# Two more output buffers taken from the first expert's token tile, and a flag word loaded without its bounds check

## The chip, the cores and the metric

The kernel runs on one core of a Trainium2 chip. A core has five engines that work side by side, each with its own queue of instructions: TensorE (PE, matrix products), VectorE (DVE), ScalarE (ACT), GpSimd (POOL) and SyncE (SP, which issues most of the DMAs). They wait for one another by semaphores. The metric is the device time of one execution in microseconds (us), lower is better.

## The reference

Attention, then a mixture of experts. The attention (4 batches, 8 heads, 768 positions, 64 dimensions) is masked: a query sees the keys that fall to the same of 16 centroids. Its output, 3072 tokens of 512 numbers, goes through a two-level router that sends each token to one of 16 experts with one gate per token; the expert is a two-layer net:

```python
for g in range(G):                    # 4 groups of 4 experts
    ...
    for e in range(Eg):
        mask_e = e_idx == e
        h = np.maximum(xg[mask_e] @ w1[g, e], 0.0)   # 512 -> 1024
        ye = h @ w2[g, e]                            # 1024 -> 512
        combined = g_w[mask_g][mask_e] * e_w[mask_e]
        out[tok_idx] = combined[:, None] * ye
```

## The kernel before

Attention takes the first 405 us; the experts, which overlap its end, take the rest. Each expert's tokens are gathered from DRAM by index, multiplied, and scattered to their rows of the output by index.

**The experts.** One expert, chosen early ("the first expert"), is computed in a part A with 256 tokens (line 1183) as soon as most of attention is done; its last tokens follow in a part B of at most 104 rows. The function `bridge` runs part A's second layer beside part B's first. The other 15 experts are sorted by their number of tokens, and `ranks` runs them as ranks 0 to 14, the fullest first (288 tokens for rank 0, then 272, 256, 240, 232, ...). In each round the first layer (`up`, matmuls of line 1064 into `psh`) of rank k is interleaved with the second layer (`down`, lines 1098 or 1122 into `psy`) of rank k-1.

Numbers are split into a high and a low 16-bit half, so that three 16-bit products stand for one of higher precision. Hence the names: `hh` and `hl` are the two halves of the hidden values, written from `psh` by ACT (line 1069) and then by DVE (line 1070); `wh..` and `wl..` are the two halves of a weight matrix, made of a loaded 512 KB chunk `st` by ACT (line 833) or POOL (line 835) and then by DVE (line 836). SP loads the chunks (line 826); some are loaded straight into weight buffers that are not yet in use.

**Outputs.** The function `emit` (line 1160) finishes one tile of up to 128 tokens: ACT scales PSUM by the gate into a buffer `y` of 128 x 512 in fp32 (line 1163), and POOL issues an indirect DMA that scatters its rows to the output (line 1164). `y` has three buffers, used in turn; a write to one waits until the DMA that read it three tiles earlier has landed. There are 35 such tiles: two for part A, one for part B, three each for ranks 0 and 1 (the third one of 32 and of 16 rows), and two for every other rank. Ranks in the `down` form of line 1098 keep their results (`owed`) until `settle`, in the round after, turns them through the `psm` tiles of line 1150 and emits them one behind the other; rank 2, with two tiles, has the form of line 1122 and emits each tile when its sum is finished.

**Order.** From the second half of `bridge` to the last rank the order on PE, ACT and DVE is that of the program text (`manual_schedule`); an instruction that waits holds everything behind it on its engine. POOL and SP are placed by a planner. `widen` (line 1160's change asks for it) is false in the bridge and in the first round and true from round 1 on, which is where rank 0's tiles are emitted; `again` is true only in a path for tokens left over, which this data does not enter.

**The first expert's tokens.** `fetch` (lines 905 to 944) puts part A's 256 tokens, transposed, into the tile `xTA`: 128 partitions with 4 x 2 x 256 fp16 numbers, that is 4096 bytes each. Part A's first layer reads it; its last matmul of that kind starts at 403.5 us.

**The word of flags.** For most ranks the program holds two versions of each group of matmuls, a wide and a narrow one, and PE branches between them (line 1304) by a bit of a register `word`. At step 5 of the bridge's second loop (line 1457) `values_load` loads this register on PE from SBUF. With it come instructions that test the value against its declared bounds.

Of the kernel before, what the change touches and what calls it, by code (L numbers as in the profile page):

```python
# [14 lines left out]
F32 = mybir.dt.float32  # L15
# [4 lines left out]
ET = mybir.EngineType  # L20
# [4 lines left out]
P = 128  # L25
# [720 lines left out]
class Experts:  # L746
# [155 lines left out]
    def fetch(self):  # L902

        nc, R, CA, KD = self.nc, self.R, self.CA, self.R.KD
        nt = -(-CA // P)
        sz = [min(P, CA - t * P) for t in range(nt)]
        tab = self.small("tabA", [P, nt, 2])
        tv = R.table.rearrange("(e s) w -> e s w", s=R.BS)[bass.ds(self.f0, 1)].rearrange("e s w -> (e s) w")
        self.nt = -(-max(self.caps) // P)
        self.tb = self.small("tb", [R.E, self.nt * P, 2])  # L910
        while R.done < R.B - 2:
            yield
        for _ in range(READ + 2):
            yield
        with self.after(), self.tc.issue_after(self.cfg["mr"].ins) if "mr" in self.cfg else ExitStack():
            for t, n in enumerate(sz):
                R.reads(nc.sync.dma_start(out=tab[0:n, t], in_=tv[t * P:t * P + n]))
            R.reads(nc.sync.dma_start(out=self.tb, in_=R.table.rearrange("(e s) w -> e s w", s=R.BS)[0:R.E, 0:self.nt * P]))
        for _ in range(READ):
            yield  # L920
        ids = self.small("idA", [P, nt], I32)
        g = self.small("gA", [P, nt])
        with self.after():
            for t, n in enumerate(sz):
                nc.vector.tensor_copy(out=ids[0:n, t:t + 1], in_=tab[0:n, t, 0:1])
                nc.vector.tensor_scalar(out=g[0:n, t:t + 1], in0=tab[0:n, t, 1:2], scalar1=1.0 / (XS * WS * WS), scalar2=None, op0=ALU.mult)
        self.colsA = [g[0:n, t:t + 1] for t, n in enumerate(sz)], [ids[0:n, t:t + 1] for t, n in enumerate(sz)]

        rows = R.N - R.N // R.B
        xgs = []  # L930
        for t, n in enumerate(sz):
            xf = self.cfg["ld"].tile([P, KD * P * 3 // 2], F32, name=("qx", "kx", "vx")[t])[:, 0:self.D]
            nc.vector.memset(xf, 0.0)
            xgs.append(xf.bitcast(F16).rearrange("p (k a x) -> p k a x", a=2, x=P))
            if rows:
                with self.tc.issue_after(self.cfg["los"][0].ins) if "los" in self.cfg else ExitStack():
                    self.gather(ids[0:n, t:t + 1], n, xgs[t], rows)
            for _ in range(2):
                yield
        xTA = self.wa.tile([P, KD, 2, CA], F16, name="xTA")  # L940
        self.xTA = xTA.rearrange("p k a m -> p a k m")
        for t, n in enumerate(sz):
            nc.sync.dma_start_transpose(out=xTA.rearrange("p k a m -> p (k a) m")[:, :, t * P:t * P + n], in_=xgs[t][0:n].rearrange("p k a x -> p (k a x)"))
            yield

    def open(self, ctx):
        tc = self.tc
        late = ctx.enter_context(tc.tile_pool(name="econst2", bufs=1))
        self.small = lambda name, shape, dt=F32: late.tile(shape, dt, name=name)
        self.stage2 = ctx.enter_context(tc.tile_pool(name="stage2", bufs=2))  # L950
        wp = ctx.enter_context(tc.tile_pool(name="wp", bufs=1))
        self.W = [[self.wtiles(wp, 0, n) for n in "ab"], [self.WA[2:4], self.wtiles(wp, 1, "b")]]
        self.xp = ctx.enter_context(tc.tile_pool(name="mxp", bufs=2))
        self.pinned, self.left, self.widen = False, None, False
        self.owed, self.wrote, self.again = [], [], False
        self.back = late.tile([P, P], F16, name="back")
        self.nc.vector.tensor_scalar(out=self.back, in0=self.cfg["ident"], scalar1=YS, scalar2=None, op0=ALU.mult)
        self.ps_y = ctx.enter_context(tc.tile_pool(name="ps_y", bufs=2, space=PSUM))
# [200 lines left out]

    def emit(self, py, n, g, idc):  # L1160
        nc = self.nc
        y = self.xp.tile([P, self.D], F32, name="y", bufs=3)
        nc.scalar.activation(out=y[0:n], in_=py[0:n, 0:self.D], func=AF.Copy, scale=g)  # L1163
        d = self.put = nc.gpsimd.indirect_dma_start(  # L1164
            out=self.out, out_offset=bass.IndirectOffsetOnAxis(ap=idc, axis=0),
            in_=y[0:n], in_offset=None, bounds_check=self.R.N - 1, oob_is_err=False)
        if self.again:
            self.R.behind(d, self.wrote)
        else:

            self.R.alone(d, "wrote", self.wrote)
# [263 lines left out]
    def bridge(self, ga, new):  # L1435

        for i in range(8):
            next(ga)
            with self.tc.issue_after(self.mm.ins):
                if i >= self.ADD:  # L1440
                    next(new, None)
        self.pinned = True
        with self.tc.manual_schedule(engines=PINNED):
            h = []
            up = None
            for i in range(8):
                next(ga)
                if self.left:
                    self.left()
                    self.left = None  # L1450
                for _ in range((2, 1, 0, 1)[i] if i < 4 else 0):
                    next(new, None)
                if i == 0:
                    self.xTB = self.tokens_b()
                    up = self.up(self.xTB, self.CB, self.WA[0:2], h)
                if i == 5:
                    self.word = self.nc.values_load(self.wi[0:1, 0:1], engines=[ET.PE], min_val=0, max_val=2 ** self.R.E - 1)
                for _ in range(self.BESIDE[i]):
                    next(up)
                if i == self.SLOTS:  # L1460
                    self.slots()
                if i >= self.SLOTS:
                    next(self.fill)
            for _ in ga:
                pass
            xT = self.tokens(self.xg0, self.caps[0])
            for _ in up:
                next(self.fill)
            self.settle()
        return xT, self.xg0, None, self.down(h, self.CB, self.WA[2:4], [self.gB], [self.idB])  # L1470
# [238 lines left out]
```

## Time and profile before

| | |
|---|---|
| time, 3 runs | median 713.98 us (713.72 to 715.66) |
| profiled execution | 716.25 us, of which its span (first to last instruction) 714.4 us |
| busy share of the span | PE 96%, DVE 81%, ACT 70%, POOL 64% |
| mean granted TensorE clock | 0.992 |
| chain that ended last | PE 64%, DVE 14%, ACT 9%, DMA 6%, issue 5% |
| DMA | 136.74 MB, mean 191 GB/s |

All times of the rows below are microseconds from the start of the span. A duration in a row is that of the group of like instructions that the row stands for, and "x12" is their number. "Idle before" is how long the engine had nothing to do before that instruction, and the name behind the arrow is what ended this idle time. "issue" is idle time in which the engine waited for nothing that the profile shows. A row of a stretch holds, after its length, the busy time of PE, PEld (PE's weight loads), DVE, ACT and POOL with their numbers of instructions, then the granted clock as a share of 2.4 GHz, the busy share of the 16 DMA engines, and GB/s. A queue name with a q (SPq, PEldq) stands for instructions that the engine's sequencer carries out itself.

### The profile page before, as it was taken

How to read it: one execution, taken by the hardware profiler on the slowest of the kernel's cores; microseconds unless marked ns; L12 is line 12 of the kernel's file. 1: busy time of each engine (PE TensorE's matmuls, PEld its weight loads, DVE VectorE, ACT ScalarE, POOL GpSimd, SP SyncE). 2: the span in 40 equal slices, each digit the busy share in tenths (PEclk: the TensorE clock that was granted, in tenths of full speed). 3: DMA queues.
4: the chain of work that ended last, by engine and by line, in shares of the span. 5: the costliest groups of instructions: out<-in, count | busy, mean ns of one | idle time of the engine just before them, and what ended most of it. 6: DMA issues, size and time to landing. Idle time of an engine off the chain costs nothing.

```text
span 714.4 us, 25953 instructions
## 1 busy us (share of the span) xinstructions
PE 683.5 (96%) x10528; PEld 585.7 (82%) x10528; DVE 581.4 (81%) x1226; ACT 500.5 (70%) x948; POOL 459.4 (64%) x522
## 2 busy tenths in 40 slices
PE   5989999999999999999999989999899999999996
PEld 3667887887788887887778857898599999999995
DVE  5998989899798998989887836768488788888961
ACT  5558898897888978977996336665446666667642
POOL 9768888899988999989985032324524254453442
PEclk9999999999999999999999999999999999999998
DMA  8765737557486474552755179899789899888721
GB/s 254 201 176 158 201 89 189 136 125 196 96 167 157 110 203 100 116 120 52 167 119 106 61 265 313 283 353 226 279 257 293 272 289 302 300 286 294 217 78 48
DMA packets 89528, 136.74 MB, mean 191 GB/s; under 512 B 41508, under 2 KB 59428, under 8 KB 89385
## 3 DMA queue, kind: packets, MB, share of 16 engines
q1 hardware_dynamic: 83884, 121.32, 61.0%
q0 software_dynamic: 5344, 13.38, 5.6%
q8 instruction: 102, 1.67, 1.0%
q14 instruction: 42, 0.34, 0.2%
q10 hardware_dynamic: 156, 0.03, 0.0%
HBM read 93.17 MB, written 13.99 MB: 150 GB/s over the span
## 4 chain that ended last, share of the span: by engine, by line
PE 64%; DVE 14%; ACT 9%; DMA 6%; issue 5%; POOL 1%; SPq 1%; POOLq 0%; ACTq 0%; DVEq 0%
PE psh L1064 15%; PE psy L1098 14%; PE pso L395 10%; PE psc L320 6%; PE psf L362 5%; PE psf L363 5%; DVE mpart L323 5%; ACT p L367 3%; PE psy L1122 2%; PE psm L253 2%; DMA xT<-xg 1%; PE psm L1150 1%; PE psm L1032 1%; DMA vx<-vr 1%; DMA out_dram<-y,ri 1%
## 5 line engine op out<-in xcount | busy, mean ns | idle before, releaser
L374 POOL TENSOR_TENSOR pl<-p 128x512 f16<-128x512 f32 x193 | 198.8, 1055 | 20.3 <-ACT p L367 19.1
L323 DVE TENSOR_REDUCE mpart<-psc 128x1 f32<-128x512 f32 (+1 forms) x282 | 188.4, 681 | 17.8 <-PE psc L320 16.0
L367 ACT ACTIVATE p<-psf 128x512 f32<-128x512 f32 x288 | 171.8, 599 | 41.5 <-PE psf L363 33.6
L395 PE MATMUL pso<-V,pl 128*128 128x65 f16 (+1 forms) x1968 | 161.0, 193 | 0.0
L362 PE MATMUL psf<-A 82*128 82x384 f16 (+2 forms) x576 | 143.9, 274 | 2.3 <-ACT p L367 0.8
L363 PE MATMUL psf<-B 128*128 128x384 f16 (+2 forms) x576 | 143.7, 274 | 0.0
L395 PEld LDWEIGHTS <-pl 128*128 128x128 f16 x1968 | 130.9, 97 | 1.8 <-issue 0.4
L395 PEld LDWEIGHTS <-p 128*128 128x128 bf16 x1632 | 112.4, 98 | 20.3 <-issue 0.5
L395 PE MATMUL pso<-V,p 128*128 128x65 f16 x1632 | 120.8, 193 | 0.0
L374 POOL TENSOR_TENSOR pl<-p,ph 128x512 f16<-128x512 f32 x84 | 96.8, 1161 | 24.8 <-POOL pl L374 9.6
L320 PE MATMUL psc<-A 80*128 80x512 f16 (+1 forms) x376 | 107.6, 331 | 4.4 <-DVE mpart L323 3.0
L1069 ACT ACTIVATE hh<-psh 128x256 f16<-128x256 f32 (+14 forms) x136 | 46.1, 346 | 79.6 <-PE psh L1064 61.6
L1022 POOL DMA_INDIRECT xg<-xbuf,ri x32 | 35.1, 1098 | 84.2 <-PE psm L1032 38.4
L1070 DVE SCALAR_TENSOR_TENSOR hl<-psh,hh 128x256 f16<-128x256 f32 (+14 forms) x136 | 47.0, 365 | 36.3 <-ACT hh L1069 34.1
L1064 PE MATMUL psh<-xT,wh0a 128*128 128x272 f16 (+14 forms) x512 | 66.0, 246 | 3.2 <-DVE hl L1070 3.0
L363 PEld LDWEIGHTS <-B 128*128 128x128 f16 x576 | 56.8, 99 | 13.5 <-issue 4.1
L362 PEld LDWEIGHTS <-A 82*128 82x128 f16 x576 | 56.0, 98 | 10.3 <-issue 1.8
L1064 PE MATMUL psh<-xT,wl0a 128*128 128x272 f16 (+7 forms) x256 | 59.5, 245 | 0.0
L1064 PE MATMUL psh<-xT,wh0b 128*128 128x272 f16 (+6 forms) x448 | 57.2, 245 | 0.1
L1164 POOL DMA_INDIRECT out_dram<-y,ri x32 | 40.2, 1256 | 22.1 <-ACT y L1163 14.9
L371 ACT CAST ph<-p 128x512 f16<-128x512 f32 x84 | 51.9, 617 | 2.3
L1064 PE MATMUL psh<-xT,wl0b 128*128 128x240 f16 (+6 forms) x224 | 52.3, 244 | 0.0
(328 smaller groups left out, 1607.8 us busy)
## 6 DMA issues: line engine op xcount, KB each, us to landing
st<-w SPq DMA_DIRECT2D x88, 512.0 KB
B<-parts SPq DMA_DIRECT2D x64, 192.0 KB
wh<-w SPq DMA_DIRECT2D x21, 512.0 KB
wl<-w SPq DMA_DIRECT2D x19, 512.0 KB
kx<-kT SPq DMA_DIRECT2D x16, 384.0 KB
qx<-qT SPq DMA_DIRECT2D x16, 384.0 KB
vx<-vr SPq DMA_DIRECT2D x16, 384.0 KB
A<-parts SPq DMA_DIRECT2D x32, 192.0 KB
```

The costliest lines, as they stand in the source:

```text
L320: last["mm"] = nc.tensor.matmul(out=pc[:, off:off + k1 - k0], lhsT=QA[h % 8][0:80, c * P:(c + 1) * P], rhs=KA[h % 8][0:80, k0:k1], start=T ...
L323: nc.vector.tensor_reduce(out=(mp[:, 0, 0:1], mp[:, :, 1], mp[:, 1, 0:1])[i], in_=pc.rearrange("p (a x) -> p a x", a=n), axis=AX.X, op=ALU ...
L362: nc.tensor.matmul(out=o, lhsT=KA[h % 8][0:82, ks], rhs=QA[h % 8][0:82, q0:q1], start=True, stop=False)
L363: nc.tensor.matmul(out=o, lhsT=KBs[h][:, ks], rhs=QBs[h][:, q0:q1], start=False, stop=True)
L367: cfg["exp"] = nc.scalar.activation(out=p32, in_=pf, func=AF.Exp, scale=QK / (SQ * SQ))
L371: nc.scalar.copy(out=ph, in_=p32)
L374: lo = (nc.vector if u in (EARLY if h < 2 else DVE_LO[h % 8] if h < NH - 2 else DVE_END[h - NH]) else nc.gpsimd).tensor_tensor(out=pl, in0 ...
L395: nc.tensor.matmul(out=O[:, col:col + v.shape[-1]], lhsT=p[:, bs], rhs=v, start=c == 0 and q == 0 and i == 0, stop=c == NCH - 1 and i == l ...
L1064: self.mm = nc.tensor.matmul(out=ph[:, 0:n], lhsT=w[:, k, f * P:(f + 1) * P], rhs=xT[:, a, k, 0:n], start=i == 0, stop=i == 3 * KD - 1)
L1069: nc.scalar.activation(out=hh[:, f], in_=ph[:, 0:M], func=AF.Relu)
L1070: self.ev = nc.vector.scalar_tensor_tensor(out=hl[:, f], in0=ph[:, 0:M], scalar=0.0, in1=hh[:, f], op0=ALU.max, op1=ALU.subtract)
L1098: self.mm = nc.tensor.matmul(out=py[:, 0:n], lhsT=w[:, f, d * P:(d + 1) * P], rhs=a[:, f, 0:n], start=i == 0, stop=i == len(prods) - 1)
```

## The change

The first of four edits gives the bytes of `xTA` a second view, two buffers of 128 x 512 in fp32. The second adds a counter of emitted tiles. By the third, `emit` uses these two views for every tile whose number is 0 or 1 modulo 5, once `widen` is true, and the three old buffers for the others; a buffer then comes round after five tiles in place of three. No memory is added. By the fourth, the load of the word of flags is made without the check of its bounds.

```diff
--- before.py
+++ after.py
@@ -939,6 +939,7 @@
                 yield
         xTA = self.wa.tile([P, KD, 2, CA], F16, name="xTA")
         self.xTA = xTA.rearrange("p k a m -> p a k m")
+        self.yown = xTA.rearrange("p k a m -> p (k a m)").bitcast(F32)[:, 0:2 * self.D].rearrange("p (t d) -> p t d", d=self.D)
         for t, n in enumerate(sz):
             nc.sync.dma_start_transpose(out=xTA.rearrange("p k a m -> p (k a) m")[:, :, t * P:t * P + n], in_=xgs[t][0:n].rearrange("p k a x -> p (k a x)"))
             yield
@@ -951,7 +952,7 @@
         wp = ctx.enter_context(tc.tile_pool(name="wp", bufs=1))
         self.W = [[self.wtiles(wp, 0, n) for n in "ab"], [self.WA[2:4], self.wtiles(wp, 1, "b")]]
         self.xp = ctx.enter_context(tc.tile_pool(name="mxp", bufs=2))
-        self.pinned, self.left, self.widen = False, None, False
+        self.pinned, self.left, self.widen, self.ny = False, None, False, 0
         self.owed, self.wrote, self.again = [], [], False
         self.back = late.tile([P, P], F16, name="back")
         self.nc.vector.tensor_scalar(out=self.back, in0=self.cfg["ident"], scalar1=YS, scalar2=None, op0=ALU.mult)
@@ -1159,7 +1160,11 @@
 
     def emit(self, py, n, g, idc):
         nc = self.nc
-        y = self.xp.tile([P, self.D], F32, name="y", bufs=3)
+        self.ny += 1
+        if self.widen and not self.again and self.ny % 5 < 2:
+            y = self.yown[:, self.ny % 5]
+        else:
+            y = self.xp.tile([P, self.D], F32, name="y", bufs=3)
         nc.scalar.activation(out=y[0:n], in_=py[0:n, 0:self.D], func=AF.Copy, scale=g)
         d = self.put = nc.gpsimd.indirect_dma_start(
             out=self.out, out_offset=bass.IndirectOffsetOnAxis(ap=idc, axis=0),
@@ -1454,7 +1459,7 @@
                     self.xTB = self.tokens_b()
                     up = self.up(self.xTB, self.CB, self.WA[0:2], h)
                 if i == 5:
-                    self.word = self.nc.values_load(self.wi[0:1, 0:1], engines=[ET.PE], min_val=0, max_val=2 ** self.R.E - 1)
+                    self.word = self.nc.values_load(self.wi[0:1, 0:1], engines=[ET.PE], min_val=0, max_val=2 ** self.R.E - 1, skip_runtime_bounds_check_because="a sum of distinct powers of two below 2 ** E")
                 for _ in range(self.BESIDE[i]):
                     next(up)
                 if i == self.SLOTS:
```

## Rows read from the trace of the kernel before

**Rows 1.** Busy time in stretches (us, instructions), granted clock, DMA share

```profile
420.00:440.00 20.00, 16.78 (x152) 12.14 (x151) 12.24 (x20) 11.73 (x21) 8.72 (x8) 0.91 0.79 264
...
500.00:520.00 20.00, 16.99 (x140) 12.14 (x138) 10.55 (x14) 9.13 (x17) 10.76 (x11) 0.98 0.75 260
...
540.00:600.00 60.00, 59.94 (x753) 59.52 (x751) 49.49 (x77) 39.13 (x73) 24.63 (x28) 1.00 0.92 292
```

**Rows 2.** Waits of PE from 405 us on: us, times, longest

```profile
PE psh L1064 <- issue: 3.2, 6, 1.1
PE psh L1064 <- DVE hl L1070: 3.0, 1, 3.0
```

**Rows 3.** The chain of waits, 495 to 560 us: start, us, what

```profile
505.22 7.39 DMA out_dram<-y,ri
...
512.69 0.07 ACT y L1163
...
518.21 1.38 PE psh L1064 x12
519.59 3.76 PE psy L1098 x24
...
525.51 2.23 PE psy L1098 x24
```

**Rows 4.** ACT in order of time, 500 to 522 us: start, us, what

```profile
506.73 0.37 ACT L1069 ACTIVATE hh<-psh 128x240 f16<-128x240 f32 x1 [0.75 <-issue]
512.69 0.69 ACT L1163 ACTIVATE y<-psy,rg 128x512 f32<-128x512 f32 x1 [5.58 <-DMA out_dram<-y,ri]
...
515.17 0.62 ACT L1069 ACTIVATE hh<-psh 128x240 f16<-128x240 f32 x2
```

**Rows 5.** PE in order of time, around 504 us

```profile
504.08 0.38 PE L1122 MATMUL psy<-wh1b,hl 128*128 128x512 f16 x1
```

**Rows 6.** PE in order of time, around 515 us

```profile
511.27 0.26 PE L1064 MATMUL psh<-xT,wl0b 128*128 128x216 f16 x1
...
514.94 0.25 PE L1064 MATMUL psh<-xT,wl0a 128*128 128x208 f16 x1
```

**Rows 7.** Forms of line 836: duration in ns, least, median, most

```profile
L836 DVE SCALAR_TENSOR_TENSOR wl0b<-wl,wh0b x4: 1210/1216/3480, 514.4 to 629.0; 128x1024 f16<-128x1024 f32 x4
```

**Rows 8.** POOL in order of time, 508 to 520 us

```profile
514.66 2.10 POOL L835 TENSOR_SCALAR wh1b<-st 128x1024 f16<-128x1024 f32 x2
```

**Rows 9.** Busy time in the two stretches at half clock

```profile
427.03:430.45 3.42, 3.42 (x29) 2.83 (x28) 3.18 (x5) 2.77 (x6) 0.15 (x1) 0.50 0.70 196
...
519.19:522.60 3.41, 3.41 (x22) 2.88 (x20) 3.41 (x6) 2.25 (x3) 0.00 (x0) 0.50 0.85 260
```

**Rows 10.** Line 1457, what PE's sequencer did: duration in ns, start

```profile
L1457 PEldq TENSOR_LOAD <-wi x1: 487/487/487, 418.8 to 418.8; - x1
L1457 PEldq FUSED_REGOPS  x1: 170/170/170, 419.4 to 419.4; - x1
L1457 PEldq SEQ_ASSERT  x1: 28/28/28, 419.7 to 419.7; - x1
```

**Rows 11.** The chain of waits, 414 to 432 us

```profile
418.29 0.55 PE psh L1064 x12
...
421.98 0.09 PE psh L1064 x2
...
426.36 1.77 PE psy L1122 x6
```

**Rows 12.** Waits of ACT from 405 us on

```profile
ACT y L1163 <- PE psm L1150: 9.4, 9, 1.4
ACT hh L1069 <- remote: 6.2, 2, 5.9
ACT y L1163 <- DMA out_dram<-y,ri: 5.6, 1, 5.6
```

**Rows 13.** Line 861, what SP's sequencer did

```profile
L861 SPq SEQ_ASSERT  x16: 5/18/33, 339.1 to 438.3; - x16
```

## The prediction

> **What bounds the kernel now.** I began with the page: PE is busy for 96% of the span, so what the change can win is what PE loses now, wherever an edit reaches it. The edits touch nothing before 400 us. The table of stretches from there on shows where PE loses: about 20.0 of 20 us almost everywhere, but 16.78 in 420 to 440 and 16.99 in 500 to 520, and 59.94 of 60 in 540 to 600 with the DMA engines at 0.92 [rows 1]. The waits of PE put names to it: one wait of 3.0 us for DVE's `hl`, and six pauses called "issue", 3.2 us in all [rows 2]. Nothing there is a wait for a weight, a token or an output. So there are two places. Each is followed by a stretch at 0.50 of full clock, the lower of the two levels (1.2 in place of 2.4 GHz): 3.42 us from 427.03 and 3.41 us from 519.19 [rows 9].
>
> **Place 1, the buffers (edits one to three).** The chain of waits is to be read backwards from PE's first matmuls after the pause, at 518.21 [rows 3]. They wait for `hl` of an earlier group; DVE was late with it because of a weight split (line 836) that began at 514.4 and took 3.48 us in place of 1.22 [rows 7]; this split waited for ACT's half of the same weights, which stood behind the `y` at 512.69; and that waited for a scatter issued on POOL at 505.22, 7.39 us earlier [rows 3]. ACT had been idle for 5.58 us [rows 4].
>
> Why that scatter? Count the tiles from part A on: A has numbers 1 and 2, B 3, rank 0 4 to 6, rank 1 7 to 9. Rank 2's first is number 10. With three buffers it needs that of number 7, rank 1's first, whose scatter lands at 512.6. The 16-row third tile of rank 1 takes a turn as well, so the buffer comes round in the very next round. It is the one such wait in the trace: 5.6 us, once [rows 12].
>
> With the edits number 10 gets the first of the two new buffers (10 modulo 5 is 0), last used by number 5 of rank 0, whose `y` was written at about 481, over 25 us earlier. The other condition of that `y` is its sum in PSUM. Rank 2's first tile has 24 matmuls (8 blocks of hidden values by 3 products); the PE timeline from 495.33 on gives 12, then 6, then 6, and the last of these ends at 504.08 + 0.38 = 504.46 [rows 5]. So `y` can start when ACT is through with `hh`, at 506.73 + 0.37 = 507.1 [rows 4], 5.6 us earlier.
>
> What is late next? Behind `y` stand two weight splits of ACT, about 1.05 us each, then two `hh`; those were one block to 515.17 + 0.62 [rows 4] and can move by up to 5.6 us, held then only by PE, whose second group for them ends at 511.27 + 0.26 = 511.5 [rows 6]. The two `hl` would be ready at about 511 and 512. PE asks for the first at 514.94 + 0.25 = 515.2 [rows 6]. Some 3 us of room stand against a stall of 3.0 us, so I take the whole stall: **3.0 us**. Where the new start of `y` is not quite 507, it may be 3 us later without cost.
>
> The half clock after it goes with the pause, as I read it: PE ran without a break and at full clock for some 85 us before it, and the fall came 4 us after the pause began. At 0.50, 3.41 us do the work of 1.7: **1.7 us**. The rows bear this out: 24 matmuls of line 1098 take 3.76 us at 519.59 and 2.23 at 525.51 [rows 3], 1.53 of it. Bounds of this place: from 0 (another wait takes its turn at the same point) to 4.7; I take 4.7.
>
> Is it given back later? PE then reaches each later point 4.7 us earlier, and whoever feeds it moves with it: SP's loads are released by DVE's splits, POOL's gathers by PE. With DMA at 0.92 and PE at 59.94 of 60 [rows 1] PE's pace doesn't rise, it only starts earlier, and so the loads keep their lead. The last ranks' `y` don't wait for buffers: the waits of ACT give 9.4 us in nine for the PE tiles of line 1150 [rows 12]. So the end moves with PE. In rank 0, where the new buffers serve first, the three old ones were free in time too; there is nothing to win.
>
> What the edits add: no instruction, no byte. The scatters of tiles 5 and 6 read other addresses; part A's last read of them began at 403.5.
>
> **Place 2, the check (edit four).** PE's sequencer spends 0.487 us on the load of the register, 0.170 and 0.028 on the two instructions that can only be the check [rows 10]: the edit takes out 0.2 us, or 0.36 with the gaps around them (from 419.33 to 419.68). Before this the array had work queued, and its group after it starts on time, so directly the check costs **0**.
>
> But the pauses follow close behind. A group of 12 matmuls takes 0.55 us at 418.29; the one that begins at 421.98 is only through at 426.36, 4.38 us, 3.8 too many [rows 11]; with the half clock after it (3.42 us, of which half is lost) that is 5.5. And ACT waited 5.9 us for `psh` with a releaser that the profile calls remote, one of two such waits [rows 12]. If the check does this, edit four is worth 5.5 us; if not, nothing. For it: it is the one place where PE carries out such instructions. Against it: the group that ACT waited for ends by the chain at 418.29 + 0.55 = 418.84, before the first instruction of the check at 419.4 [rows 10, 11], so its signal was late for a cause that came first: the register load itself, the six semaphore waits before it, or POOL's seven DMA issues back to back, all of which stay. And SP passes 16 such asserts of 18 ns [rows 13], with no stall that the waits show. The bounds are 0 and 5.5; a loss is excluded, since a queue only becomes shorter. By the nearer row, the order in time at 418.84, I take 0.
>
> **The sum.** 716.25 us (the profiled execution; its span and 1.85 around it) - 3.0 - 1.7 - 0 = 711.5. The median of the runs is 2.27 us below the profiled execution; with that it is **709.3**.
>
> **The rivals.**
> (a) Both places go. The check stops PE's signals and with them its supply; without it ACT's `hh` starts at about 418.9 and DVE's splits, and so the loads, some 5 us earlier, so that the gain is carried on. 713.98 - 4.7 - 5.5 = 703.8. Its weak point is the order in time above. Chance 0.28, against 0.45 for the forecast.
> (b) The pause at 515 only shrinks. DVE's slow split at 514.4 exceeded its usual time by 3.48 - 1.22 = 2.26 us, and POOL's two splits beside it took 2.10 [rows 7, 8]. If the `hl` in question stays behind a split that meets these two, up to 2.26 us of the 3.0 remain, and 0.7 to 2.4 are won: 711.6 to 713.3, say 712. Against it: POOL's pair begins at 514.66, after both `hl` of my sum. Chance 0.08. (The Trainium skill, "SBUF — State Buffer", section "Who interferes with whom", says that a DVE instruction with two SBUF inputs contends with a GpSimd one that reads SBUF and that the later one fully blocks; the trace agrees with the 2.26 beside the 2.10. By that rule alone, any split that starts just ahead of or inside POOL's pair loses up to 2 us, wherever the pair ends up.)
> (c) Neither place moves PE: 714. It would need a second reason for ACT's idle time, such as a chunk landing at 512 as well. The waits name only the scatter, but a wait for several is put down to the last. Chance 0.10.
> (d) Slower: the two new buffers are halves of one tile. If their writes and scatters are ordered as those of one tile, the second of a pair that is emitted together waits for the first one's scatter. Such pairs are numbers 5 and 6, 20 and 21, 30 and 31 (10 and 11 lie several us apart). A wait of 5.58 us on ACT cost 4.7 at place 1, so three would cost up to 14.1, less the 4.7 won: 723, or 716 if half is covered. It decides at ACT's third `y` of rank 0, at about 481: it must not wait for a DMA. Against it: other weight and token tiles of this kernel are written and read by parts, and PE's waits show no trace of that. With lesser mishaps (the planner moves an instruction of POOL or SP in front of a gather) 0.09.
>
> **How the numbers follow.** A measurement of this kernel can tell about 0.3%, 2.1 us, from no change. The forecast, 709.3, has 0.45 and a range of its own of 708.3 to 711, since the runs of before spread by 1.9. Faster by over 0.3%, that is below 711.8: the forecast, (a) and half of (b), and less than all of each by chance of the runs, 0.77; within: 0.14; slower: 0.09. For 8 in 10 the range must take in (a), whose end is 703.8, and go up to (b) and a part of (c): 703.2 to 713.6.
>
> **What would show it.** Place 1: in the chain around 505 to 520 no scatter, ACT's first `y` of rank 2 right behind `hh` at about 507, no wait of PE for `hl` and a clock of 1.00 in 500 to 540. If ACT's `y` starts early and PE still pauses at 515, the step on what is late next is wrong; if the pause goes and the half clock stays, the step on the clock. Place 2: no test instructions at line 1457, but pauses of about 3 us between 421 and 427 with ACT's 5.9 us wait and the half clock at 427; if these are gone, (a) holds and my step from the order in time is what failed. Wrong altogether: a median of 713 or more with ACT's wait at 512 gone.

## The result

The changed kernel: **705.25 us** (704.71 to 705.83, 5 executions), where the kernel before stood at 715.66 (713.72 to 716.15, 5); ratio 0.9867, 95% interval 0.9848 to 0.9887. The forecast was 709.3, its range 703.2 to 713.6.

This first pair flatters the change. In later comparisons, each on one chip, the kernel before is no kernel of 714 us: in three of the four, 77 executions of it lie anywhere between 703.3 and 718.2, median 712.3; in the fourth, beside e9, 17 executions lie between 712.0 and 725.3, median 719.7. The changed kernel, run again beside it (a2 below), had 705.55 (704.10 to 707.80, 12) against 710.88 (703.33 to 718.16, 17). Ratios of fast runs leave out executions over 1.5% above the fastest of the same kernel, which here cuts off the upper part of the kernel before and nothing of the changed one (a2's ratio is then 0.9987, 0.9959 to 1.0014, which shows no difference), so medians over all executions are compared below. The fastest executions of both lie within 1.5 us of each other: what the change takes away is the upper part of the kernel before.

The profile after, of an execution of 705.2 us (span 703.4). First the waits of PE from 405 us on: who waited for what, us in all, times, longest.

```profile
PE psh L1065 <- DMA st<-w: 1.0, 1, 1.0
PE psh L1065 <- ACT xT L1035: 0.5, 1, 0.5
PE psh L1065 <- DVE xT L1035: 0.2, 1, 0.2
```

Both entries of [rows 2] are gone; the largest is now 1.0 us for a weight chunk (it ends at 543.4 us). ACT in order of time at rank 2 (start, us, what):

```profile
498.85 0.37 ACT L1070 ACTIVATE hh<-psh 128x240 f16<-128x240 f32 x1 [0.75 <-PE psh L1065]
499.12 0.68 ACT L1168 ACTIVATE xTA<-psy,rg 128x512 f32<-128x512 f32 x1
499.69 1.06 ACT L833 ACTIVATE wh0b<-wl 128x1024 f16<-128x1024 f32 x1
...
502.56 0.37 ACT L1070 ACTIVATE hh<-psh 128x240 f16<-128x240 f32 x1 [0.87 <-PE psh L1065]
```

In [rows 4] ACT stood idle for 5.58 us between the first two of these. Now rank 2's first output (the buffer appears under the name of the tile that it is cut from, `xTA`) follows `hh` at once, and the next `hh` waits for PE alone, as the forecast had it. The chain of waits runs through PE without a break:

```profile
503.64 2.59 PE psy L1123 x12
506.24 2.16 PE psh L1065 x24
508.40 2.23 PE psy L1099 x24
```

Against [rows 3]: the 24 matmuls that took 3.76 us take 2.23. The stretches (columns as in [rows 1]) have no half clock any more:

```profile
420.00:440.00 20.00, 19.29 (x190) 14.80 (x189) 14.05 (x22) 13.32 (x23) 9.54 (x8) 1.00 0.99 336
...
500.00:520.00 20.00, 20.00 (x203) 17.85 (x202) 14.91 (x23) 10.75 (x18) 6.35 (x6) 1.00 0.80 285
```

And the other place, in the chain:

```profile
415.21 0.55 PE psh L1065 x12
...
418.90 0.55 PE psh L1065 x12
419.45 1.29 PE psy L1123 x6
```

The group that took 4.38 us in [rows 11] takes 0.55. Comparing the same matmuls in the two profiles: PE is 3.1 us earlier before the bridge's word of flags (attention, which no edit touches), 4.8 more after the pauses there, 4.85 more after rank 2; it gives back 1.1 at the wait for the chunk and wins 0.7 between 560 and 600, and the last matmul ends 12.3 us earlier. The end of the span comes 11.0 earlier: from POOL's last scatter on, the changed kernel took 1.3 us longer in this execution.

So place 1 is as forecast. What made place 2 go, with 3.1 us of attention besides, is what the experiments had to find.

### The profile page after: what moved, and what is told of

The parts are those of the page before. It is cut to its first block, busy times and chain, and to the rows that moved or that the text cites. A ratio compares the mean times of both kernels' runs of the same rounds, so it can differ in the third digit from the quotient of the medians.

```text
span 703.4 us, 25950 instructions
## 1 busy us (share of the span) xinstructions
PE 676.3 (96%) x10528; PEld 582.3 (83%) x10528; DVE 580.7 (83%) x1226; ACT 501.8 (71%) x948; POOL 461.3 (66%) x522
## 4 chain that ended last, share of the span: by engine, by line
PE 71%; DVE 13%; ACT 9%; issue 4%; DMA 2%; POOL 1%; POOLq 0%; DVEq 0%; SPq 0%; ACTq 0%
PE psh L1065 17%; PE psy L1099 14%; PE pso L395 11%; PE psf L362 6%; PE psc L320 6%; PE psf L363 6%; DVE mpart L323 5%; PE psy L1123 4%; ACT p L367 3%; PE psm L1151 2%; PE psm L253 2%; ACT ph L371 1%; PE psm L1033 1%; PE psm L633 1%; ACT psm L853 1%
## 5 line engine op out<-in xcount | busy, mean ns | idle before, releaser
L1023 POOL DMA_INDIRECT xg<-xbuf,ri x32 | 37.8, 1180 | 75.5 <-PE psm L1033 30.2
L320 PEld LDWEIGHTS <-A 80*128 80x128 f16 x384 | 37.4, 99 | 15.9 <-issue 6.3
```

The source lines that it names most:

```text
L320: last["mm"] = nc.tensor.matmul(out=pc[:, off:off + k1 - k0], lhsT=QA[h % 8][0:80, c * P:(c + 1) * P], rhs=KA[h % 8][0:80, k0:k1], start=T ...
```

## The experiments

Theory A: the two places are separate, and the check is worth what place 2 lost. Theory B: place 2 has nothing to do with the check. Times in us, median (range, executions); each line beside the kernel before on the same chip at the same time. The edits of e1, e3, e4, e5, e8 and e9 are against the changed kernel, those of e2 and e7 against the kernel before; the code is shortened.

```
kernel                                  median (range, n)              kernel before
e1  two more buffers, check kept        704.98 (704.24..707.38, 12)    712.26 (703.91..718.16, 35)
e2  three buffers, no check             706.90 (703.69..716.42, 12)    as e1
e3  all edits, check kept, later        705.27 (703.74..708.07, 12)    as e1
e4  all edits, a register operation     706.43 (704.30..708.57, 12)    as e1
e5  one more buffer, no check           705.12 (703.21..707.37, 10)    712.51 (704.71..717.53, 25)
e7  three buffers, POOL held up         712.14 (708.98..715.26, 10)    as e5
e8  five buffers, POOL held up          711.94 (710.50..712.89, 10)    as e5
e9  rank 2's two tiles only, check      714.58 (711.95..716.78, 12)    719.70 (712.04..725.25, 17)
a2  the changed kernel                  705.55 (704.10..707.80, 12)    710.88 (703.33..718.16, 17)
b1, b2, b3  the kernel before, profiled 712.70, 718.64, 715.52 (one each)
```

**e1, the buffers alone.**

```diff
-self.word = self.nc.values_load(..., max_val=2 ** self.R.E - 1, skip_runtime_bounds_check_because="...")
+self.word = self.nc.values_load(..., max_val=2 ** self.R.E - 1)
```

> The buffers alone (edits one to three; the check of bounds stays). Theory A (the two edits are worth about 4.8 us each, and each is independent of the other): the pauses of PE between 415 and 427 and ACT's wait of about 5.9 us behind line 1462 are still there, with the half clock after them, and the scatter wait at rank 2 is gone; 709 to 711 us where the kernel before stands at 714 to 716. Theory B (the pauses come from something else that varies from one execution or one build to the next, and the check has nothing to do with it): no pauses here either, 704.5 to 706.

704.98: theory A falls, B holds. The order of instructions on every queue is that of the kernel before. The check was carried out (sequencer rows of its line: least, median, most in ns, start):

```profile
L1462 PEldq FUSED_REGOPS  x1: 170/170/170, 417.8 to 417.8; - x1
L1462 PEldq SEQ_ASSERT  x1: 24/24/24, 418.1 to 418.1; - x1
```

and the groups behind it are on time (chain):

```profile
418.55 0.55 PE psh L1065 x12
...
420.39 0.55 PE psh L1065 x12
420.94 1.29 PE psy L1123 x6
```

**e2, the check alone taken out.**

```diff
-self.word = self.nc.values_load(..., max_val=2 ** self.R.E - 1)
+self.word = self.nc.values_load(..., max_val=2 ** self.R.E - 1, skip_runtime_bounds_check_because="...")
```

> The check alone taken out (edit four; three output buffers stay). Theory A: no pauses of PE between 415 and 427 and no half clock there, but the scatter wait of ACT at rank 2, the pause of 3.0 us and the half clock after it stay; 709.5 to 711. Theory B: 709.5 to 716, with or without the pauses. A third reading, that the two gains share one cause (a PE that is 4.8 us earlier at rank 2 changes what the scatter meets): the scatter wait is then longer or shorter than 5.6 us by some us.

Neither forecast fits: the time is spread as widely as that of the kernel before, from 703.69 to 716.42. Its profile is of a short execution (705.24) and shows why there are short ones. ACT still waits for the scatter:

```profile
504.26 0.69 ACT L1163 ACTIVATE y<-psy,rg 128x512 f32<-128x512 f32 x1 [3.38 <-DMA out_dram<-y,ri]
```

but PE has no wait for `hl`. A wait of 3.4 us costs nothing. It is 2.2 us shorter than in the profile before, as the third reading allows, but the kernel before itself has waits of 2.5 to 7.9 (below). One thing stays open: the median, 706.90, is 5.4 us below that of the kernel before, and 6 of the 12 executions lie under 706.5, where the kernel before has 5 of 35. With so wide a spread 12 executions don't decide whether the short wait comes more often without the check.

**e3, the check kept but some 4 us later**, and **e4, a register operation in its place.**

```diff
 # e3                                     # e4
-if i == 5:                               +self.word = self.nc.snap((self.word * 4 + 3) >> 2,
-    self.word = self.nc.values_load(...) +                         engines=[ET.PE])
 ...
 for _ in ga: pass
+self.word = self.nc.values_load(..., max_val=2 ** self.R.E - 1)
```

> All four edits but the check stays, and the load of the word of flags with its check stands some 4 us later, behind the second loop of the bridge, where POOL's seven back-to-back DMA issues are over. Theory A1 (the check stops PE's signals or its supply wherever it stands): pauses of PE behind the new place and ACT waiting on a signal that is late, 3 to 6 us lost against all four edits: 708 to 711. Theory A2 (the check hurts only where it meets POOL's DMA issues and the small matmuls of the bridge): no such pause, 704.5 to 706.5.

> All four edits, and one register instruction on PE behind the load of the word (times 4, plus 3, shifted right by 2: the word itself) in the place of the two of the check. Theory C1 (any register instruction of that kind on PE there, or the length of PE's program, makes the pauses): 708 to 711 with the pauses. Theory C2 (it is the assert instruction): no pauses, 704.5 to 706.5.

705.27 and 706.43, both without the pauses at place 2: A2 and C2 as far as they go, but since e1 has none either, these two tell no more than that neither the place nor the kind of instruction costs anything that 12 executions show (e4's 1.2 us above e3 lies within the spread of a few us that all of them have).

**b1, the kernel before again.** Unchanged.

> The kernel before once more, unchanged, for a second profile of it. Theory A (its time varies because rank 1's first scatter lands sooner or later, and ACT's y at rank 2 waits for it): PE pauses at rank 2 by about as much as the time is above 704 to 706, give or take 1.5 us for the start and the last half clock; no pauses between 415 and 427. Theory B (the pauses between 415 and 427 come back with the kernel before and make half of its excess): these pauses again, with ACT waiting over 5 us there.

A. Waits of PE, then of ACT, then DVE's slow split (in order of time):

```profile
PE psh L1064 <- DVE hl L1070: 4.3, 1, 4.3
```

```profile
ACT y L1163 <- DMA out_dram<-y,ri: 6.9, 1, 6.9
```

```profile
509.58 3.47 DVE L836 SCALAR_TENSOR_TENSOR wl0b<-wl,wh0b 128x1024 f16<-128x1024 f32 x1 [6.96 <-ACT wh0b L833]
```

There are no pauses at place 2, though the check is there. The chain above it: SP's transpose of tokens (`xT<-xg`, 12.2 us under the load of weight chunks) holds POOL's gather, POOL's gather holds the scatters queued behind it, and rank 1's first scatter goes out at 501.36.

**e5, one more buffer in place of two.**

```diff
-if self.widen and not self.again and self.ny % 5 < 2:
-    y = self.yown[:, self.ny % 5]
+if self.widen and not self.again and self.ny % 4 < 1:
+    y = self.yown[:, 0]
```

> All four edits, but with one more buffer in place of two: tiles whose number is 0 modulo 4 go to the new buffer, so that a buffer comes round after four tiles. Theory A (what counts is that rank 2's first tile, number 10, does not need the buffer of number 7): like the changed kernel, 704 to 708 in every execution, no wait of ACT for a scatter. Rival (the gain needs the fifth buffer, or comes from elsewhere in the change): scatter waits at another tile, some executions above 709.

705.12, none above 707.4, and ACT waits for no scatter: four buffers do.

**e7 and e8, POOL held up.** The kernel before (e7) and the changed one (e8) with

```diff
+if self.ny == 7:
+    for _ in range(12):
+        m = nc.gpsimd.tensor_copy(out=self.pad, in_=y[:, 0:256])
+    self.pads = m.ins
+# and tc.issue_after(self.pads) around the scatters of tiles 7 to 9
```

> The kernel before (three buffers, check kept) with 12 copies of 128 x 256 on POOL, about 3.6 us, put between rank 1's y and its scatters. Theory A: the scatter lands some 3.6 us later and ACT's y at rank 2 with it; beyond the 2.5 to 3 us that PE can stand each us costs PE one, so median 3 to 5 us above the kernel before on the same chip, 714 to 717, and no execution near 704. Rival (the spread of the kernel before has nothing to do with rank 1's scatter): no more than 1 us above it.

> The changed kernel (five buffers) with the same 12 copies on POOL at the same place. Theory A: POOL is late by the same 3.6 us, but nobody waits for rank 1's scatter; like the changed kernel, 704 to 708. Rival (the lateness of POOL itself, its weight splits and gathers behind the scatters, is what costs): 3 us or more above the changed kernel, 708 to 711.

My sizes were off, and the rival of e8 holds. The 12 copies took 7.3 and 9.0 us, not 3.6. In e7 the low end moved up by 4.3 us (708.98 against 704.71) as A said, but the median did not move, as its rival said. The scatter went out late, but it also landed sooner:

```profile
505.82 2.78 DMA out_dram<-y,ri
```

against 7.39 in [rows 3] and 6.47 in b1; the DMA engines were busy for 0.25 of these 2.78 us, and for 0.99 and 0.98 of the other two stretches. In e8 nobody waited for a scatter, and yet it lost some 6.8 us against e5: POOL's own weight split came so late that DVE waited for it (in order of time), and PE for what stood behind that:

```profile
516.58 2.06 DVE L836 SCALAR_TENSOR_TENSOR wl1b<-st,wh1b 128x1024 f16<-128x1024 f32 x1 [5.39 <-POOL wh1b L835]
```

```profile
PE psh L1066 <- DVE hl L1072: 2.4, 1, 2.4
```

So the pair can't weigh the scatter wait by itself. e7's profile is useful in another way: POOL's two splits moved apart, and DVE's split behind the wait took its usual time:

```profile
510.37 1.23 DVE L836 SCALAR_TENSOR_TENSOR wl0b<-wl,wh0b 128x1024 f16<-128x1024 f32 x1 [8.89 <-ACT wh0b L833]
```

```profile
PE psh L1065 <- DVE hl L1071: 4.0, 1, 4.0
```

with a wait of ACT of 8.8 us:

```profile
ACT y L1165 <- DMA out_dram<-y,ri: 8.8, 1, 8.8
```

DVE's next split, which met the second one of POOL, is the slow one here, but the `hl` that PE waited for stands ahead of it:

```profile
512.21 2.44 DVE L836 SCALAR_TENSOR_TENSOR wl0b<-st,wh0b 128x1024 f16<-128x1024 f32 x1
```

That gives the law of place 1. From [rows 4, 6, 7]: a wait of 5.58 us gave a pause of 3.0, of which 3.48 - 1.22 = 2.26 are the split that met POOL's pair; the rest, 0.75, is the wait less 4.8 us of room. e7, without that meeting, gives 8.8 - 4.0 = 4.8 again. b1: 6.9 - 4.8 + 2.26 = 4.4, measured 4.3. e2: 3.4 is under 4.8, so 0, measured 0.

**b2 and b3, the kernel before twice more.** Unchanged; the law was put down first.

> The kernel before, unchanged, for a third profile. The profiles so far give PE's pause at rank 2 as ACT's wait for the scatter less 4.8 us, plus 2.3 us where DVE's weight split meets POOL's pair (waits of 3.4, 5.6, 6.9 and, in the kernel with POOL's copies, 8.8 us gave pauses of 0, 3.0, 4.3 and 4.0). Theory A: the same sum here, within 0.3 us, and half of 3.4 or 6.8 us of half clock after a pause. Rival: a pause without a wait of that size, or pauses between 415 and 427 again.

> The kernel before, unchanged, for a fourth profile; expected as for the third.

b2: a wait of 7.9 should give 7.9 - 4.8 + 2.26 = 5.4. Waits of PE, of ACT, and the split:

```profile
PE psh L1064 <- DVE hl L1070: 5.3, 1, 5.3
PE psh L1064 <- issue: 2.2, 5, 0.5
```

```profile
ACT y L1163 <- DMA out_dram<-y,ri: 7.9, 1, 7.9
ACT hh L1069 <- remote: 5.4, 2, 4.4
```

```profile
515.69 3.48 DVE L836 SCALAR_TENSOR_TENSOR wl0b<-wl,wh0b 128x1024 f16<-128x1024 f32 x1 [7.97 <-ACT wh0b L833]
```

b3 has a wait of 2.5 and no pause for `hl`:

```profile
ACT y L1163 <- DMA out_dram<-y,ri: 2.5, 1, 2.5
```

Both agree. But b2's second rows show place 2 back, with its pauses and its late signal, as the second half of the rival had it: against the same matmuls of the changed kernel's profile PE lost 4.4 us there in b2 and 4.3 in b3. The same was so in e9, which ran with them (4.4). b3 and e9 lost another 1.5 and 1.7 us just ahead of that, in a stretch of 3.41 us at half clock that began at 415.2 in both, over 5 us before the load of the word of flags (at 420.9 and 420.4). That part can't come from the check.

**e9, only rank 2's two tiles in the new buffers**, the check kept (put back as in e1), every queue in the order of the kernel before.

```diff
-if self.widen and not self.again and self.ny % 5 < 2:
-    y = self.yown[:, self.ny % 5]
+if self.ny in (10, 11):
+    y = self.yown[:, self.ny - 10]
```

> The kernel before, check included and every queue in the same order, in which only rank 2's two tiles (numbers 10 and 11) go to the two new buffers; all other tiles turn in the three old ones. Theory A (the whole effect of the change, its lower median and its narrower spread, is one wait at rank 2's first tile): like the changed kernel, median 704.5 to 706, no execution above 709. Rival (other buffer waits, or pauses that come and go elsewhere, carry part of the spread up to 718): a median of 707 to 711 and executions above 710.

The level is some 9 us above A's, and that of the kernel before is higher as well (fastest 712.04, elsewhere 703.3 to 704.7), but the shape is A's: ACT waits for no scatter, the spread shrinks from 13.2 us to 4.8, the median falls by 5.1, and the low end stays (711.95). The wait for a buffer at rank 2 carries most of the spread of the kernel before.

**a2, the changed kernel again**, for whether place 2 needs the check under the condition of b2, b3 and e9.

> The changed kernel, unchanged, beside the kernel before on the same chip. In the last three profiles, all with the check, PE lost some 4.4 us behind the load of the word of flags again and no execution of the kernel before was under 712; in the ones before that, with and without the check, it lost nothing there. Theory C (where this loss is about, it needs the check): if the kernel before again stays above 711 here, the changed kernel stays at 704 to 707 and its profile has no late signal of PE between 415 and 427. Theory S (the loss belongs to the chip's condition at the time, with or without the check): if the kernel before stays above 711, the changed kernel is at 711 to 715 and its profile shows the loss at the same place. If the fastest executions of the kernel before come near 704, this run says nothing on the check, and the changed kernel is at 704 to 707.

The kernel before went down to 703.33 here, so the condition was not met and the run says nothing on it. It gives the plainest measure of the change: medians 710.88 and 705.55, 5.3 us.

**What the condition is.** The four profiles with the loss at place 2 (that of before, b2, b3, e9) also share a small wait in attention that the other ten do not have. Waits of PE from 160 to 300 us, in b2:

```profile
PE psc L320 <- DVE mpart L323: 1.1, 3, 0.5
PE psm L275 <- DVE oh L265: 0.5, 2, 0.3
```

and in b1, the same kernel:

```profile
PE psc L320 <- DVE mpart L323: 1.4, 2, 0.7
```

Attention is 1.4 to 2.2 us longer between 158 and 294 us in the four (the same matmuls, in the order before, b2, b3, e9: 2.2, 1.8, 1.5, 1.4 us against the changed kernel; b1: 0.0). It lies ahead of the check, and one and the same kernel has it or not. So the first pair of profiles compared the kernel before under this condition with the changed one without it. All four have the check, and no kernel without the check was profiled under the condition, so whether the loss at place 2 also needs the check stays open. Under the common condition the check costs nothing measurable in kernels with five buffers.

## Why the prediction was right, and where not

**Place 1, what waits for what: right.** Rank 2's first `y` waited for the scatter of rank 1's first tile because of three buffers; with four (e5), with five, and with only rank 2's tiles moved (e9), the wait goes and with it most of the spread.

**Place 1, the room: under-estimated.** I took "some 3 us of room" for a wait of 5.6. The room is 4.8 us, by two profiles that agree (before, e7), and the pauses of b1 and b2 follow from it. Of the 3.0 us, 2.26 were the meeting of DVE's split with POOL's pair, which I had only as rival (b). Had the pair been elsewhere, the same wait would by this law have cost 0.75. (The Trainium skill, "SBUF — State Buffer", section "Who interferes with whom", has a DVE instruction with two SBUF inputs contend with a GpSimd one that reads SBUF; 3.47 and 3.48 us in before, b1 and b2 against 1.23 in e7 agree.) That the later of the two is the one that waits, as my rival (b) had it, the trace doesn't show: DVE's split began at 514.4, POOL's pair at 514.66 [rows 7, 8], and it is DVE's, the earlier one, that took longer.

**Place 1, the clock: right.** The profiles with a pause of PE at rank 2, from 2.4 us (e8) to 5.3 (b2), have a half clock behind it, 3.41 us long (6.83 in e7); those without a pause have none there. Pause and clock together: 4.85 us in the trace, forecast 4.7.

At place 2 the clock doesn't follow so simply: b2's pauses there, 2.7 us in all, have no half clock behind them.

**Place 1, its size as a term of the sum: right in the pair, but priced from one execution.** In the two profiles it came out as forecast. But I took the wait of one execution as the kernel's. The wait was 2.5, 3.4, 5.6, 6.9 and 7.9 us in five profiles of kernels with three buffers, hence pauses from 0 to 5.3. Taken away, it moves the median by 5.1 (e9) to 7.3 us (e1), and by 5.3 (a2) and 7.4 (e5) with the check gone too, and leaves the fastest executions where they were.

**The level that it was taken from: wrong, and that the range held is luck.** This is the step behind the 4 us by which the forecast was high. I took 4.7 off 713.98 as if all the rest were fixed. But in the profiles the changed kernel was 7.9 us further ahead even before place 1 (3.1 from the start through attention, 4.8 at place 2), and lost 1.1 of its whole lead at the chunk and 1.3 at the end. Attention no edit touches, and place 2's loss came and went with the condition, which I hadn't foreseen. The range reached down to 705.25 only because it took in rival (a), whose reason the runs don't bear out.

**Place 2, the check at 0: right under the common condition, with five buffers.** With three, e2 leaves it open. e1 and e3 carry it and are at 704.98 and 705.27, the changed kernel and e5 don't and are at 705.12 to 705.55. The argument was the order in time, a late signal older than the check. But that the pauses would stay in the profile after was wrong: they came and went with the condition. By my own sign their absence was to speak for (a); it doesn't, since they are absent in e1 too, with the check in place. Rival (a) named a time close to the measured one (703.8), for a reason that e1 contradicts in 12 executions.

**Given back later: nearly right.** 1.1 us went to a wait for a weight chunk; a2's profile has it too, 1.3 us. That PE meets it because it comes earlier isn't shown: e1 has no such wait, and b3, with the kernel before, has one of 1.4 us.

**Rival (d): no.** The new buffers' tiles never wait for a scatter. Rank 0's second and third tile, the two halves, are written one behind the other, without idle time and before either is scattered (at 475.45 and 477.44):

```profile
472.82 1.23 ACT L1168 ACTIVATE xTA<-psm,rg 128x512 f32<-128x512 f32 x2
```

## What to carry to other kernels

Count how many turns a rotating buffer is given, in the time that its DMA takes to land including all that its issuing queue is waiting for, and remember that a small last tile takes a turn like a full one. What a wait costs is the wait less the room behind it, plus what the late start runs into; here one to one beyond 4.8 us. Before a stall of one profile is priced, profile the unchanged kernel a few times on more than one occasion: what comes and goes by itself would otherwise be booked to the change.

## What was not expected of the hardware

The scatter of rank 1's first tile took 6.5 to 7.5 us to land (before, b1, b2), with the DMA engines busy for 0.97 to 0.99 of that time, and 2.8 us in e7, with 0.25; most of the spread of a whole kernel over 15 us hung on it. Twelve like copies of 128 x 256 on POOL took 7.3 us in one kernel and 9.0 in another, most 0.40 us each and some 1.17 to 1.41. And one program has two conditions in which its attention differs by 1.4 to 2.2 us and its bridge by 4.4 to 6.1; what sets them, no run here shows.
